# Attention block on one core: the loop's matmuls issued as two column tiles of 64

## The chip, the cores and the metric

The kernel runs on one core of a Trainium2 chip. The metric is the device time of one execution in microseconds (us); lower is better. The engines that matter are TensorE (PE, matmuls, with its weight loads listed apart as PEld), VectorE (DVE), ScalarE (ACT), GpSimd (POOL) and the queue of SyncE (SP), which here only issues DMAs. [...] A matmul holds one operand (the weights) in TensorE's array and streams the other (the moving operand) through it. The columns of the weights become the partitions of the result in PSUM. Each matmul in the program is a weight load and a matmul for the engine.

## What is computed

```
x (8, 112, 640), k_cache and v_cache (8, 32, 512, 192), wq (640, 6144), wo (6144, 640), all bf16
q = (x @ wq).reshape(B, Sq, H, Dh).transpose(0, 2, 1, 3)
scores = einsum("bhqd,bhkd->bhqk", q, k_cache) * Dh ** -0.5
p = softmax(scores)
o = einsum("bhqk,bhkd->bhqd", p, v_cache)
return o.transpose(0, 2, 1, 3).reshape(B, Sq, H * Dh) @ wo
```

## The kernel before

The work is cut into 128 pairs of heads: 4 groups of 8 heads, 8 batches in each, 4 pairs in each batch. A loop of periods runs over the pairs, and each engine has a fixed list of stages for a period, each with a lag, written out by hand (`DEFAULT_ORDERS`, lines 12 to 18). There is no scheduler: a stage waits on semaphores and then issues its instructions in order. For pair `i`, TensorE's list is S(i), PT0(i-1), PV(i-2), PT1(i-1), O(i-3), Q(i+2).

- **S** (`pe_S`, L166 to L169): scores of the two heads, four matmuls each. The weights are q (112 columns), the moving operand is a K tile with 256 elements a partition.
- **PT0, PT1** (`pe_PT`, L182): transposes the exponentials of one head and scales them, by four matmuls against a diagonal matrix `dg` (112 moving elements, 128 columns of weights).
- **PV** (`pe_PV`): the weights are V, the moving operand the transposed probabilities, 112 elements. A head has 192 channels. The first 128 run in L200 as full-width matmuls, eight a pair. The last 64 run in L206 with 64 columns: head 0 writes PSUM partitions 0 to 63, head 1 partitions 64 to 127, alternating, eight a pair.
- **O** (`pe_O`, L234 and L235): multiplies by wo, three times 512 and 128 moving elements, 112 columns of weights.
- **Q** (`pe_Q`, L262): projects x with wq for a later pair, 15 matmuls with 112 moving elements and 128 columns.

At the start `pe_xt` (L402) transposes x.

VectorE's list for a period: the scaled copy and row minimum of the scores of both heads (L332), four copies that lay q out (L323 to L326), the copy of one transposed head from PSUM (L338), reciprocals (L344), two diagonals (L308), and, once in four pairs, two instructions that add the output to `acc` (L373 to L377). ScalarE empties PSUM for Q, PT0 and PV (L272, L278, L291) and does the exponentials (L284).

K and V come from DRAM in 64 groups of four heads, that is of two pairs. SP issues them in turn: a transposing DMA for K (L477), then a DMA for V (L489). Each has six buffers. The K DMA of a group waits until the scores of the group six before it are done, the V DMA until PV of that group is. The weights wq and wo are issued by POOL, paced by waits on the K that has landed. [...]

An instruction carries a tile size and a tile position in the array. Before, all matmuls have the size 128x128, save those of L206: these have 128 rows by 64 columns, at column 0 or 64.

## Time and profile before

| | |
|---|---|
| time, median of 3 runs | 501.38 us (500.34 to 502.07) |
| span of the profiled execution | 499.2 us |
| granted TensorE clock, mean | 0.999 |
| matmuls, and as many weight loads | 6824 |
| ACT, share of the span busy | 71% |
| DMA moved | 119.90 MB, 240 GB/s in the mean |
| K transposes (L477), 64 | median 9.9 us from issue to landing |

A profile is one execution of the program, taken on the chip. The page gives busy times of each engine, a strip of the span in 40 slices, the DMA queues, the chain of waits that ended last, and the costliest groups of instructions. Matmuls are pipelined, so one matmul's listed duration, for example 213 ns in L200, is longer than the step to the next; steps are read from starts. In the list of groups, a row gives line, engine, operation, output and inputs, shapes, count, then total busy time and mean ns of one, then the idle time of the engine before them and what ended it. In the timeline, a row gives start and duration in us, engine, line, operation and how many were merged (x4). In the list of DMA queues the columns are packets, MB and share of 16 engines.

### The profile page before, as it was taken

To read this page: it belongs to the slowest core of one execution; us is meant where nothing else is said; L and a number is where in the kernel's file an instruction comes from. 1 tells how busy PE (TensorE), PEld (TensorE's weight loads), DVE (VectorE), ACT (ScalarE), POOL (GpSimd) and SP (SyncE) were. 2 spreads that over 40 slices of the span, in tenths; PEclk is the share of its full clock that TensorE was granted. 3 is DMA by queue.
4 is the path that set the end of the run, shared out by engine and by line. 5 is a ranking of instruction groups with operands and counts; after the bars stand their busy time and mean duration, and the time that the engine had idled before them with its cause. 6 is when DMAs were issued, how large, how long until landed. Compare 5 with 4: busy or idle time off the path is not lost.

```text
span 499.2 us, 18678 instructions
## 1 busy us (share of the span) xinstructions
PE 479.0 (96%) x6824; PEld 418.9 (84%) x6824; DVE 446.6 (89%) x1610; ACT 355.1 (71%) x898; POOL 71.5 (14%) x133
## 2 busy tenths in 40 slices
PE   1799999999999999999999999999999999999995
PEld 1788888888888888888888888888888888888884
DVE  2589999998999999999999999999999999999994
ACT  1277777777777777777777777777777777777773
POOL 7110133131000133131000122322000000000000
PEclk9999999999999999999999999999999999999999
DMA  9999999999999999999999999999999999999000
GB/s 227 305 285 239 244 256 274 249 265 292 237 249 263 281 261 259 245 265 251 239 247 236 259 290 279 240 282 260 233 272 254 255 260 255 238 258 261 3 14 25
DMA packets 239738, 119.90 MB, mean 240 GB/s; under 512 B 201840, under 2 KB 236480, under 8 KB 239648
## 3 DMA queue, kind: packets, MB, share of 16 engines
q1 hardware_dynamic: 233472, 101.82, 94.4%
q0 software_dynamic: 6176, 16.88, 11.3%
q8 instruction: 56, 0.92, 0.8%
q14 instruction: 34, 0.28, 0.2%
HBM read 67.21 MB, written 1.15 MB: 137 GB/s over the span
## 4 chain that ended last, share of the span: by engine, by line
PE 93%; DMA 2%; issue 1%; DVE 1%; POOL 1%; ACT 0%; DVEq 0%; POOLq 0%; ACTq 0%
PE ps L262 19%; PE ps L234 16%; PE ps L182 13%; PE ps L200 10%; PE ps L206 8%; PE ps L166 6%; PE ps L169 6%; PE ps L167 6%; PE ps L168 6%; PE ps L235 4%; DMA wq_sb<-in_wq_dram 2%; DVE xT_sb L409 1%; POOL wq_sb L578 0%; DVE s_sb L332 0%; DVE o_out L377 0%
## 5 line engine op out<-in xcount | busy, mean ns | idle before, releaser
L284 ACT ACTIVATE p_sb<-s_sb,nmx 112x512 bf16<-112x512 f32 x256 | 181.6, 712 | 3.1 <-DVE s_sb L332 2.1
L332 DVE TENSOR_SCALAR_CACHE_REDUCE s_sb<-ps 112x512 f32<-112x512 f32 x256 | 166.3, 686 | 16.2 <-PE ps L169 14.0
L278 ACT ACTIVATE pT_sb<-ps 128x448 bf16<-128x448 f32 x128 | 69.5, 543 | 88.4 <-PE ps L182 88.4
L262 PE MATMUL ps<-xT_sb,wq_sb 128*128 128x112 bf16 x1920 | 118.0, 215 | 5.2 <-DMA wq_sb<-in_wq_dram 5.2
L234 PE MATMUL ps<-wo_sb,oT_sb 128*112 128x512 bf16 x384 | 118.3, 380 | 0.0
L262 PEld LDWEIGHTS ps<-xT_sb,wq_sb 128*128 128x128 bf16 x1920 | 103.8, 99 | 16.7 <-DMA wq_sb<-in_wq_dram 4.4
L182 PE MATMUL ps<-dg,p_sb 112*128 112x112 bf16 x1024 | 94.0, 214 | 1.8 <-ACT p_sb L284 1.6
L272 ACT ACTIVATE qs<-ps 128x336 bf16<-128x336 f32 x128 | 57.6, 450 | 45.0 <-PE ps L262 41.8
L338 DVE CAST pT_sb<-ps 128x448 bf16<-128x448 f32 x128 | 79.9, 624 | 5.3 <-PE ps L182 1.4
L235 PE MATMUL ps<-wo_sb,oT_sb 128*112 128x128 bf16 x384 | 83.9, 219 | 0.0
L182 PEld LDWEIGHTS ps<-dg,p_sb 112*128 112x128 bf16 x1024 | 64.5, 98 | 14.4 <-ACT p_sb L284 1.9
L166 PE MATMUL ps<-kt,qs 128*112 128x256 bf16 x256 | 70.8, 277 | 2.5 <-issue 1.9
L200 PE MATMUL ps<-pT_sb,vt 128*128 128x112 bf16 x1024 | 71.8, 213 | 0.1
L167 PE MATMUL ps<-kt,qs 128*112 128x256 bf16 x256 | 70.4, 275 | 0.0
L169 PE MATMUL ps<-kt,qs 128*112 128x256 bf16 x256 | 70.4, 275 | 0.0
L168 PE MATMUL ps<-kt,qs 128*112 128x256 bf16 x256 | 70.3, 275 | 0.0
L234 PEld LDWEIGHTS ps<-wo_sb,oT_sb 128*112 128x112 bf16 x384 | 49.7, 129 | 22.3
L581 POOL DMA_DIRECT2D wq_sb<-in_wq_dram x60 | 32.1, 539 | 188.5 <-DMA kt<-in_k_cache_dram 182.4
L308 DVE TENSOR_SCALAR dg<-ident,rinv 112x112 bf16<-112x112 bf16 x256 | 52.9, 249 | 5.0 <-issue 0.5
L200 PEld LDWEIGHTS ps<-pT_sb,vt 128*128 128x128 bf16 x1024 | 56.5, 98 | 0.9 <-issue 0.5
L291 ACT ACTIVATE oT_sb<-ps 128x336 bf16<-128x336 f32 x128 | 55.3, 432 | 1.7 <-PE ps L206 1.7
L235 PEld LDWEIGHTS ps<-wo_sb,oT_sb 128*112 128x112 bf16 x384 | 50.0, 130 | 0.0
(38 smaller groups left out, 498.5 us busy)
## 6 DMA issues: line engine op xcount, KB each, us to landing
vt<-in_v_cache_dram SPq DMA_DIRECT2D x64, 768.0 KB, 5.8
wq_sb<-in_wq_dram POOLq DMA_DIRECT2D x60, 96.0 KB, 5.3
wo_sb<-in_wo_dram POOLq DMA_DIRECT2D x24, 160.0 KB, 5.6
wo_sb<-in_wo_dram POOLq DMA_DIRECT2D x32, 80.0 KB, 5.1
wq_sb<-in_wq_dram POOLq DMA_DIRECT2D x4, 480.0 KB, 10.2
wo_sb<-in_wo_dram POOLq DMA_DIRECT2D x4, 320.0 KB, 10.9
out_dram<-o_out SPq DMA_DIRECT2D x8, 140.0 KB, 4.4
kt<-in_k_cache_dram SPq DMA_TRANSPOSE x64, 9.9
```

What stands on the lines that cost most here:

```text
L166: pe.matmul(bk[:, 0:256], qs[:, qb, EA[h], :], ktb[:, :, 0, cs], start=True, stop=False)
L167: pe.matmul(bk[:, 0:256], qs[:, qb, ET[h], :], ktb[:, :, 1, cs], start=False, stop=True)
L168: pe.matmul(bk[:, 256:512], qs[:, qb, OC[h], :], ktb[:, :, 2, cs], start=True, stop=False)
L169: pe.matmul(bk[:, 256:512], qs[:, qb, OH[h], :], ktb[:, :, 1, cs], start=False, stop=True).then_inc(sS, 1)
L182: mm = pe.matmul(ps[:, 2 + h, j * SQ:(j + 1) * SQ], p_sb[:, pslot, j * 128:(j + 1) * 128], dg[:, dslot, :], start=True, stop=True)
L200: pe.matmul(ps[:, 4, oc * SQ:(oc + 1) * SQ], vtb[:, u, q * 192: q * 192 + 128], pT_sb[:, ptb, h, j * SQ:(j + 1) * SQ], start=(j == 0), sto ...
L234: pe.matmul(ps[0:SQ, 6, :], oT_sb[:, ob, c, :], wo_sb[:, wb, 3 * lp + c, 0:512], start=first, stop=last)
L235: mm = pe.matmul(ps[0:SQ, 7, 0:128], oT_sb[:, ob, c, :], wo_sb[:, wb, 3 * lp + c, 512:640], start=first, stop=last)
L262: mm = pe.matmul(ps[:, 5, c * SQ:(c + 1) * SQ], lhsT, xT_sb[:, dc, b * SQ:(b + 1) * SQ], start=(dc == 0), stop=(dc == DC - 1))
L284: act.activation(p_sb[:, Hh % NP, :], s_sb[:, Hh % NSS, :], ACTF.Exp, bias=nmx[:, Hh % NS:Hh % NS + 1], scale=-1.0, accum_out=rsum[:, Hh % ...
L332: dve.tensor_scalar(s_sb[:, Hh % NSS, :], ps[0:SQ, h, :], -scale, None, op0=ALU.mult, op1=ALU.min, accum_out=nmx[:, Hh % NS:Hh % NS + 1]). ...
L338: dve.tensor_copy(pT_sb[:, ip % NPT, 1, :], ps[:, 3, 0:4 * SQ]).then_inc(dPTE, 1)
```

## The change

A helper `mmc` issues a matmul as two: columns 0 to 63 of the weights into PSUM partitions 0 to 63, then the rest into the partitions from 64 on. Both have the same moving operand. It is used in S, PT0, PT1, the L200 part of PV, O and Q. Where the weights have 112 columns the second tile has 48, else 64. The alternating matmuls of L206 stay as they are, and so do the transposes at the start. The semaphore is still signalled by the last matmul of a stage. The program then has 12584 matmuls, all with tile size 128x64 but the 40 of the start. No other engine's code changes.

```diff
+        def mmc(pe, out, lhsT, rhs, start, stop, m):
+            for a in (0, 64):
+                e = min(a + 64, m)
+                mm = pe.matmul(out(a, e), lhsT(a, e), rhs, start=start, stop=stop)
+            return mm
...
-                bk = ps[0:SQ, h, :]
...
-                pe.matmul(bk[:, 0:256], qs[:, qb, EA[h], :], ktb[:, :, 0, cs], start=True, stop=False)
...
+                mmc(pe, lambda a, e: ps[a:e, h, 0:256], lambda a, e: qs[:, qb, EA[h], a:e], ktb[:, :, 0, cs], True, False, SQ)
...
-                mm = pe.matmul(ps[:, 2 + h, j * SQ:(j + 1) * SQ], p_sb[:, pslot, j * 128:(j + 1) * 128],
-                               dg[:, dslot, :], start=True, stop=True)
+                mm = mmc(pe, lambda a, e: ps[a:e, 2 + h, j * SQ:(j + 1) * SQ],
+                         lambda a, e: p_sb[:, pslot, j * 128 + a:j * 128 + e], dg[:, dslot, :], True, True, 128)
...
-                    pe.matmul(ps[:, 4, oc * SQ:(oc + 1) * SQ], vtb[:, u, q * 192: q * 192 + 128],
-                              pT_sb[:, ptb, h, j * SQ:(j + 1) * SQ], start=(j == 0), stop=(j == 3))
+                    mmc(pe, lambda a, e: ps[a:e, 4, oc * SQ:(oc + 1) * SQ],
+                        lambda a, e: vtb[:, u, q * 192 + a:q * 192 + e],
+                        pT_sb[:, ptb, h, j * SQ:(j + 1) * SQ], j == 0, j == 3, 128)
...
-                pe.matmul(ps[0:SQ, 6, :], oT_sb[:, ob, c, :], wo_sb[:, wb, 3 * lp + c, 0:512], start=first, stop=last)
-                mm = pe.matmul(ps[0:SQ, 7, 0:128], oT_sb[:, ob, c, :], wo_sb[:, wb, 3 * lp + c, 512:640], start=first, stop=last)
+                mmc(pe, lambda a, e: ps[a:e, 6, :], lambda a, e: oT_sb[:, ob, c, a:e],
+                    wo_sb[:, wb, 3 * lp + c, 0:512], first, last, SQ)
+                mm = mmc(pe, lambda a, e: ps[a:e, 7, 0:128], lambda a, e: oT_sb[:, ob, c, a:e],
+                         wo_sb[:, wb, 3 * lp + c, 512:640], first, last, SQ)
...
-                    lhsT = wq_sb[:, wb, dc, c0 + 128 * c:c0 + 128 * (c + 1)]
-                    mm = pe.matmul(ps[:, 5, c * SQ:(c + 1) * SQ], lhsT, xT_sb[:, dc, b * SQ:(b + 1) * SQ],
-                                   start=(dc == 0), stop=(dc == DC - 1))
+                    w0 = c0 + 128 * c
+                    mm = mmc(pe, lambda a, e: ps[a:e, 5, c * SQ:(c + 1) * SQ],
+                             lambda a, e: wq_sb[:, wb, dc, w0 + a:w0 + e], xT_sb[:, dc, b * SQ:(b + 1) * SQ],
+                             dc == 0, dc == DC - 1, 128)
```

More of the change, by code (lines that the diff above doesn't have):

```diff
@@ L162, in pe_S @@
                 W(pe, dSM, Hh - 1)
-                bk = ps[0:SQ, h, :]
                 ktb = kt[kb]
                 cs = slice(u * 128, (u + 1) * 128)
-                pe.matmul(bk[:, 0:256], qs[:, qb, EA[h], :], ktb[:, :, 0, cs], start=True, stop=False)
-                pe.matmul(bk[:, 0:256], qs[:, qb, ET[h], :], ktb[:, :, 1, cs], start=False, stop=True)
-                pe.matmul(bk[:, 256:512], qs[:, qb, OC[h], :], ktb[:, :, 2, cs], start=True, stop=False)
-                pe.matmul(bk[:, 256:512], qs[:, qb, OH[h], :], ktb[:, :, 1, cs], start=False, stop=True).then_inc(sS, 1)
+                mmc(pe, lambda a, e: ps[a:e, h, 0:256], lambda a, e: qs[:, qb, EA[h], a:e], ktb[:, :, 0, cs], True, False, SQ)
+                mmc(pe, lambda a, e: ps[a:e, h, 0:256], lambda a, e: qs[:, qb, ET[h], a:e], ktb[:, :, 1, cs], False, True, SQ)
+                mmc(pe, lambda a, e: ps[a:e, h, 256:512], lambda a, e: qs[:, qb, OC[h], a:e], ktb[:, :, 2, cs], True, False, SQ)
+                mmc(pe, lambda a, e: ps[a:e, h, 256:512], lambda a, e: qs[:, qb, OH[h], a:e], ktb[:, :, 1, cs], False, True, SQ).then_inc(sS, 1)
         def pe_PT(pe, ip, h):
```

## Prediction

> **What bounds the kernel now.** I read the engines' shares first, then the chain of waits, then TensorE, VectorE and the DMA queue in order of time.

> ```profile
> PE 479.0 (96%) x6824; PEld 418.9 (84%) x6824; DVE 446.6 (89%) x1610; ACT 355.1 (71%) x898; POOL 71.5 (14%) x133
> ...
> PE 93%; DMA 2%; issue 1%; DVE 1%; POOL 1%; ACT 0%; DVEq 0%; POOLq 0%; ACTq 0%
> ```

> TensorE (PE) is the chain, but two others stand close behind it: VectorE (DVE) is busy 89% of the span, and the DMA row is at 9 in nearly every slice. So what the change saves on PE has to be followed until one of these takes over. In steady state one pair of heads takes 3.65 us (starts of L166 lie at 252.81 and 256.46 in the timeline, and most of the 128 steps of the trace read 3.64 to 3.65). Here is the part of such a step that holds the mixed tilings, TensorE in order of time:

> ```profile
> 253.69 0.36 PE L182 MATMUL ps<-dg,p_sb 112*128 112x112 bf16 x4
> 253.88 0.56 PE L200 MATMUL ps<-pT_sb,vt 128*128 128x112 bf16 x8
> 254.38 0.39 PE L206 MATMUL ps<-pT_sb,vt 128*64 128x112 bf16 x8
> 254.69 0.37 PE L182 MATMUL ps<-dg,p_sb 112*128 112x112 bf16 x4
> 254.90 0.38 PE L234 MATMUL ps<-wo_sb,oT_sb 128*112 128x512 bf16 x1
> ```

> Read the starts, since the durations overlap. Four matmuls of L182 move on by 0.19 us, 49 ns each. Eight of L200 at 49 ns would be 0.39 us, but L206 starts 0.50 us later. L206 is the stage already in 64-column tiles, and the next lines show how it runs: the same eight matmuls asked for in windows that end 0.05 us apart.

> ```profile
> 254.38 0.24 PE L206 MATMUL ps<-pT_sb,vt 128*64 128x112 bf16 x2
> 254.38 0.29 PE L206 MATMUL ps<-pT_sb,vt 128*64 128x112 bf16 x4
> 254.38 0.34 PE L206 MATMUL ps<-pT_sb,vt 128*64 128x112 bf16 x6
> ```

> They start two at a time, and a pair costs what one full matmul does: the single records start at 254.375/.379, 254.449/.452, 254.498/.501 and 254.547/.550, so 49 ns a pair after a first step of 74 ns.

> **The cost of a tiling switch.** From the last L200 start (254.233) to the first L206 start (254.375) is 142 ns, 93 more than 49. The first pair's 74 ns is 25 more. From the last pair (254.547) to L182 (254.695) is 148 ns, 99 more. The step behind that, 60 ns (251.049 to 251.109 one turn earlier), is 11 more. Together 228 ns of each 3.647 us. Times 128 pairs that is 29 us, the most that the change can remove.

> **What the change adds on PE.** Each split matmul becomes two with half the columns and the same moving rows. Priced by L206 a pair at 112 moving elements is 49 ns, which is also the step of L182, L200 and L262. For 256, 512 and 128 moving elements I keep today's steps of 109, 215 and 55 ns, because they scale with the moving side, and that is unchanged. PE then needs 3.647 - 0.228 = 3.42 us a pair. Bounds of the pair's step: 49 ns from L206's second to fourth pair, 74 ns from its first, and below 49 nothing, as the moving side alone gives that in L182. I take 49, since it is the nearest row. The startup transposes of L402 stay on the full array: four changes of tiling, well under 1 us.

> Weight loads lie beside the matmuls:

> ```profile
> L262 PEld LDWEIGHTS ps<-xT_sb,wq_sb 128*128 128x128 bf16 x1920 | 103.8, 99 | 16.7 <-DMA wq_sb<-in_wq_dram 4.4 <-DVE xT_sb L409 1.8
> ...
> L167 PEld LDWEIGHTS ps<-kt,qs 128*112 128x112 bf16 x256 | 33.8, 132 | 0.0
> ...
> L206 PEld LDWEIGHTS ps<-pT_sb,vt 128*64 128x64 bf16 x1024 | 30.6, 109 | 11.6
> ```

> A 64-column load takes 109 ns against 99 for 128 columns, and 132 for 112. In L206 two such loads still fit under each 49 ns pair, so I cost them at nothing; the cover is the running pair, and without it every pair would pay some 10 ns. [...]

> Instructions on PE's queue grow from 106 to 196 a pair (53 to 98 matmuls with a load each), 17 ns each at 3.42 us. The trace's records of PE's own waits date the handing out: between one that ends at 257.463 and the next at 257.615 lie the 32 loads and matmuls of L200 and L206, so 4.8 ns each is possible, and the densest stages ask for 12.3 (49/4). No charge. [...]

> **What takes over: VectorE.** Its instructions are not touched.

> ```profile
> 253.14 0.88 DVE L375 TENSOR_TENSOR acc<-ps,acc 112x512 f32<-112x512 f32 x2
> 253.94 0.68 DVE L332 TENSOR_SCALAR_CACHE_REDUCE s_sb<-ps 112x512 f32<-112x512 f32 x1
> ...
> 257.25 0.68 DVE L332 TENSOR_SCALAR_CACHE_REDUCE s_sb<-ps 112x512 f32<-112x512 f32 x1
> ```

> From 253.94 to 257.25 DVE has no gap: 3.31 us is the least for a pair. Every fourth pair adds the sum into acc, 0.80 us (253.14 to 253.94) to 0.82. Four pairs need 4 x 3.31 + 0.82 = 14.06 us. PE needs 4 x 3.647 = 14.59 now and 13.68 after. So DVE becomes the bound at 14.06, 7.03 us for a group of two pairs (K and V come in groups of four heads), against 7.29 now. If nothing else held, 64 groups would win 64 x 0.265 = 17 us.

> **And the K stream.** K arrives by transposing DMAs on SP's queue:

> ```profile
> 331.22 7.15 SPq L477 DMA_TRANSPOSE kt<-in_k_cache_dram  x1
> 338.41 0.58 SPq L489 DMA_DIRECT2D vt<-in_v_cache_dram  x1
> 339.04 7.42 SPq L477 DMA_TRANSPOSE kt<-in_k_cache_dram  x1
> ```

> SP is back to back, 7.8 us a group here, slower than either engine will be. It doesn't wait for PE: group 46's buffer was given up by group 40's scores at about 319.4, 20 us before 339.04. So faster matmuls don't bring K sooner. By the trace's landing records, groups 10 to 14 land 0.4 us before PE starts on them (already PE's limit at 94 to 125 us); later the lead is 5 to 15 us and at the end 27. A group's start is the later of the last start plus the period, and landing plus 0.4. With 7.29 this recursion puts group 63 at 482.5 (trace: 483.5). With 7.03 it is held again around groups 30 and 45, lastly by group 46, landed at 351.2. From there on weight loads ease, K comes in about 6.1 us a group, and DVE decides.

> More PE instructions are fetched; their DMA queue is this row (packets, MB, share of 16 engines):

> ```profile
> q8 instruction: 56, 0.92, 0.8%
> ```

> The extra is 11,520 loads and matmuls at 13,648/56 = 244 a packet are 47 packets of 1.14 us (0.8% of 16 engines' 499.2 us, by 56), 3.4 us on 16 engines, 2.4 us of it before group 46. Bounds 0 (hidden) and 2.4 (the engines are full); I take 2.4, as the DMA row is at 9 there.

> **The sum.** 351.2 + 2.4 + 0.4 = 354.0 for group 46; 17 groups of 7.03 us to group 63 make 473.5; from there to the end 15.7 us now (499.2 - 483.5), less two pairs' switches 0.4: span 488.8. The runs' median lies 2.2 us above the profiled span (501.38 to 499.2), so 491.0 us. Its own range: no fetch cost and PE's 6.84 us a group give 485, a full period of 7.1 us and the uncut tail give 494.

> **Rivals.**
> 1. *The gain arrives whole.* If K lands earlier than in this one trace, DVE's bound alone gives 501.4 - 17 = 484, and PE's 29 us would give 472. For: the three runs spread by 1.7 us, so something outside PE varies. Against: back-to-back SP issue until 455 us.
> 2. *Slower: twin tiles don't keep 49 ns in long rows.* L206 shows four pairs only, just behind a drain in which the queue filled up. After the change the same load of two weight tiles per pair runs 15 pairs long in L262 and 20 long from L182 to L182. If a pair takes the 74 ns of L206's first, 35 pairs a step cost 0.875 us and regain 0.228: 128 x 0.65 = +83, 584 us. The change decides at 228/35 = 6.5 ns a pair, 55.5 ns. Against: three even steps of 49 ns.
> 3. *Slower: instructions come too slowly.* At 24.6 ns each (49/2, the densest that a row of 30 shows in L262) a pair takes 196 x 24.6 = 4.82 us, 128 x 1.17 = +150, 651 us. Against: the 4.8 ns above.
> 4. *No change.* K's stream would have to be 11 us late at group 46, 3%; fetches give 2.4.
> 5. *The switches stay,* because a 48-column piece is another tiling. The second pieces start at partition 64 as L206's do, so I give it nothing of its own; it would land with 2 or 4.

> **Chances.** Forecast 0.70, rival 1 0.08, rival 2 0.12, rival 3 0.04, rivals 4 and 5 0.06. Of this kernel's three runs, 0.3% (1.5 us) is about what can be told from no change. Faster 0.79, same 0.05, slower 0.16. 481 to 500 holds the forecast, half of rival 1 and most of the small losses of gain between; rivals 2 and 3 lie beyond it.

> **What would show it.** Gaps of 142 and 148 ns around L206 gone, every split stage in twins 49 ns apart per pair; DVE without idle time before L332 in stretches of 14.06 us per four pairs; PE idle before the first matmul of the scores, on K, in groups near 10 to 14, 30 and 45; K's last landing still at 457 to 461. Wrong would be: a pair step above 55 ns, PE idle on "issue" all along, or VectorE's operations longer than now while two tiles write.

## The result and the profile after

| | before | changed |
|---|---|---|
| time, median of 4 runs each | 500.86 us (499.67 to 502.07) | 656.25 us (649.98 to 660.28) |
| span of the profiled execution | 499.2 us | 648.2 us |
| granted TensorE clock, mean | 0.999 | 0.945 |
| instruction DMAs of TensorE's queue (16 KB each) | 56 | 101 |

The changed kernel is slower: the ratio is 1.307, with an interval of 1.302 to 1.312. The ratio leaves out the slowest run of the changed kernel, which is 1.6% above its fastest. The forecast was 491 us.

From the page of the changed kernel: busy times, the strip of the granted clock, TensorE's instruction DMAs, and the chain of waits.

```profile
PE 488.6 (75%) x12584; PEld 439.1 (68%) x12584; DVE 449.1 (69%) x1610; ACT 355.1 (55%) x898; POOL 71.4 (11%) x133
...
PEclk9899988988887899888999989999899999999999
...
q8 instruction: 101, 1.65, 1.1%
...
PE 69%; issue 24%; DVE 4%; DMA 2%; POOL 1%; ACT 0%; DVEq 0%; POOLq 0%; ACTq 0%
```

TensorE is busy only 75% of a span 149 us longer. In the chain "issue" stands at 24%, time in which an engine waits for nothing that the profile shows. Before it was 1%. The prediction had named this as a sign of being wrong. Who waited for whom (us in total, times, longest) says the same:

```profile
PEld ps L156 <- issue: 150.3, 89, 6.2
PE ps L156 <- issue: 134.1, 57, 6.1
```

All split matmuls now have the helper's line, L156. They stood still without a semaphore, 57 times, up to 6.1 us.

Did the array do what the change says? TensorE in order of time, in a stretch without such a stop (L212 is the old L206):

```profile
326.74 0.36 PE L156 MATMUL ps<-dg,p_sb 112*64 112x112 bf16 x8
326.94 0.56 PE L156 MATMUL ps<-pT_sb,vt 128*64 128x112 bf16 x16
327.33 0.36 PE L212 MATMUL ps<-pT_sb,vt 128*64 128x112 bf16 x8
327.53 0.36 PE L156 MATMUL ps<-dg,p_sb 112*64 112x112 bf16 x8
```

Starts move on by 0.20, 0.39 and 0.20 us: four, eight and four pairs of tiles at 49 ns, with no gap around L212. Steps without a stop take 3.42 us. So the switches are gone, and split pairs cost what whole matmuls did. The loss is all between the matmuls. Here is one such place, TensorE in order of time:

```profile
296.67 0.95 PE L156 MATMUL ps<-xT_sb,wq_sb 128*64 128x112 bf16 x30
300.91 0.85 PE L156 MATMUL ps<-kt,qs 128*64 128x256 bf16 x8 [3.29 <-issue]
```

The DMA strip of the stretch 297.4 to 300.9 us (40 slices of 88 ns) and its queues:

```profile
DMA  9999999999999999908000110010000099999000
...
q1 hardware_dynamic: 2144, 0.54, 115.6%
q8 instruction: 1, 0.02, 1.8%
```

Until about 299 us the DMA engines are full of K's packets. One packet of q8, TensorE's instructions, falls into the stretch: by its record it starts at 298.36, ends at 299.34, and 1.56 us later the matmuls go on. And busy times before, in and behind the stop (columns: window, its length, PE, PEld, DVE, ACT and POOL busy, then the granted clock, DMA share and GB/s):

```profile
293.32:297.40 4.08, 4.08 (x124) 3.88 (x125) 2.81 (x10) 2.54 (x7) 0.00 (x0) 1.00 1.19 288
297.40:300.90 3.50, 0.22 (x9) 0.07 (x3) 0.62 (x4) 0.64 (x2) 0.00 (x0) 1.00 1.17 159
300.90:304.40 3.50, 3.49 (x58) 3.33 (x60) 2.17 (x8) 1.37 (x4) 0.00 (x0) 0.54 0.02 5
```

Behind the stop the clock is 0.54 for 3.5 us, so about half as many matmuls get through: 58 in 3.50 us (16.6 a us) against 124 in 4.08 us (30.4 a us).

**What the stops have in common.** Counting TensorE's records from the start (loads, matmuls and its wait instructions), 58 of the 59 gaps over 0.6 us (from one matmul's start to the next, after 35 us) end at an instruction number that leaves 193 or 194, once 195, when divided by 256. A packet of q8 has 16 KB, and 101 of them for 25,882 records work out at 256 instructions of 64 bytes a packet. The queue follows TensorE: its records were 14,362 before, with 56 packets, while the page's other instruction queue, q14, has 34 packets in both kernels. In each of the 58 the matmuls go on 1.2 to 1.7 us after the end of the packet that holds their block. The 59th, 1.8 us near the end, waits for the last exponentials and is in the profile before too. The 58 sum to 151 us.

### The profile page after: what moved, and what is told of

It is laid out like the page before. It is cut to its first block, busy times and chain, and to the rows that moved or that the text cites. A ratio compares the mean times of both kernels' runs of the same rounds, so it can differ in the third digit from the quotient of the medians.

```text
span 648.2 us, 30198 instructions
## 1 busy us (share of the span) xinstructions
PE 488.6 (75%) x12584; PEld 439.1 (68%) x12584; DVE 449.1 (69%) x1610; ACT 355.1 (55%) x898; POOL 71.4 (11%) x133
## 4 chain that ended last, share of the span: by engine, by line
PE 69%; issue 24%; DVE 4%; DMA 2%; POOL 1%; ACT 0%; DVEq 0%; POOLq 0%; ACTq 0%
PE ps L156 65%; PE ps L212 4%; DMA wq_sb<-in_wq_dram 2%; DVE s_sb L341 1%; DVE pT_sb L347 1%; DVE xT_sb L418 0%; DVE qs L334 0%; DVE qs L335 0%; ACT p_sb L293 0%; POOL wq_sb L587 0%; DVE dg L317 0%; DVE rinv L353 0%; DVE o_out L386 0%; DVE qs L333 0%; DVE qs L332 0%
## 5 line engine op out<-in xcount | busy, mean ns | idle before, releaser
L341 DVE TENSOR_SCALAR_CACHE_REDUCE s_sb<-ps 112x512 f32<-112x512 f32 x256 | 167.6, 688 | 119.3 <-PE ps L156 118.8
L156 PE MATMUL ps<-xT_sb,wq_sb 128*64 128x112 bf16 x3840 | 131.0, 220 | 58.9 <-issue 53.5
L156 PE MATMUL ps<-kt,qs 128*48 128x256 bf16 (+1 forms) x2048 | 146.3, 283 | 24.0 <-issue 23.3
L156 PEld LDWEIGHTS ps<-xT_sb,wq_sb 128*64 128x64 bf16 x3840 | 115.2, 115 | 72.4 <-issue 59.1
L156 PE MATMUL ps<-wo_sb,oT_sb 128*48 128x512 bf16 (+3 forms) x1536 | 139.1, 313 | 9.6 <-issue 9.6
L156 PEld LDWEIGHTS ps<-kt,qs 128*48 128x48 bf16 (+1 forms) x2048 | 112.3, 111 | 29.5 <-issue 27.4
L156 PE MATMUL ps<-dg,p_sb 112*64 112x112 bf16 x2048 | 107.9, 221 | 28.7 <-issue 26.9
L156 PEld LDWEIGHTS ps<-dg,p_sb 112*64 112x64 bf16 x2048 | 87.6, 116 | 31.0 <-issue 28.9
L156 PEld LDWEIGHTS ps<-wo_sb,oT_sb 128*48 128x48 bf16 (+1 forms) x1536 | 76.4, 112 | 35.2 <-issue 15.6
L156 PE MATMUL ps<-pT_sb,vt 128*64 128x112 bf16 x2048 | 82.2, 220 | 20.8 <-issue 20.8
L156 PEld LDWEIGHTS ps<-pT_sb,vt 128*64 128x64 bf16 x2048 | 67.3, 116 | 19.4 <-issue 19.3
L212 PE MATMUL ps<-pT_sb,vt 128*64 128x112 bf16 x1024 | 53.8, 221 | 7.9 <-issue 7.9
L212 PEld LDWEIGHTS ps<-pT_sb,vt 128*64 128x64 bf16 x1024 | 39.7, 116 | 11.5 <-issue 11.5
```

The source lines that it names most:

```text
L156: mm = pe.matmul(out(a, e), lhsT(a, e), rhs, start=start, stop=stop)
L212: mm = pe.matmul(ps[64 * h:64 * h + 64, 4, SQ:2 * SQ], vtb[:, u, q * 192 + 128: q * 192 + 192], pT_sb[:, ptb, h, j * SQ:(j + 1) * SQ], sta ...
L341: dve.tensor_scalar(s_sb[:, Hh % NSS, :], ps[0:SQ, h, :], -scale, None, op0=ALU.mult, op1=ALU.min, accum_out=nmx[:, Hh % NS:Hh % NS + 1]). ...
```

## The experiments

The table is worked out from the traces. "Block" is how long 256 instructions last at the kernel's full pace: with the waits counted, TensorE executes 112 instructions a pair before and 202 after, so 256/112 x 3.65 and 256/202 x 3.42 (the expectations say 4.46 us for the latter, without the waits). "Wait" is the time from the first instruction of a block to the start of the DMA that brings the next one, median and maximum over the run. After that come about 1.1 us of transfer and at least 1.2 us until the block runs. "Gaps" are steps of over 0.6 us from one matmul's start to the next after 35 us, number and sum.

| kernel | block, us | wait, us | gaps | time, us |
|---|---|---|---|---|
| before | 8.3 | 3.5, 6.3 | 1, 1.8 us | 500.9 |
| changed | 4.3 | 3.7, 8.3 | 59, 152.9 us | 656.3 |
| e1, changed, K's DMAs left out | 4.3 | 1.5, 6.1 | 18, 30.4 us | 512.5 |
| e2, changed, V's DMAs left out | 4.3 | 2.0, 7.4 | 31, 56.9 us | 546.2 |
| e5, changed, K's and V's left out | 4.3 | 0.9, 5.4 | 3, 6.5 us | 494.3 |
| e6, before, K's and V's left out | 8.3 | 0.5, 4.0 | 1, 1.8 us | 499.3 |
| e3, cut untiled, 202 loads and matmuls | 4.7 | 3.1, 9.0 | 50, 116.8 us | 672.6 |
| e7, cut untiled, 140 loads and matmuls | 6.5 | 3.7, 5.8 | 22, 25.8 us | 531.7 |
| e4, changed, K in four DMAs | 4.3 | 3.1, 6.5 | 60, 116.5 us | 606.6 |
| e8, PV untiled | 8.3 | 3.4, 6.1 | 2, 2.6 us | 498.7 |

**Is it the DMA traffic? e1, e2, e5 and e6.** The edits, on the changed kernel (e6: both, on the kernel before; e1, e5 and e6 also pace the weight loads by the scores):

```diff
-            W(pe, mK[kb], 16 * (g // NKB + 1))
+            W(pe, mK[kb], 16)
...
-                        issue_k(g)
+                        if g < NKB:
+                            issue_k(g)
```

```diff
-            W(pe, mV[vb], 16 * (g // NVB + 1))
+            W(pe, mV[vb], 16)
...
-                    if 0 <= g - VLAG < NGRP:
+                    if 0 <= g - VLAG < NVB:
```

> The changed kernel without K's traffic: K is loaded for the first six groups only, and later scores use those tiles again (the weight loads are paced by the scores instead of by K's landing). Theory 1, TensorE's instruction blocks (16 KB, 256 instructions, 4.46 us of work) wait behind K's bursts of 256-byte packets: a block then arrives in about 1.2 + 1.1 + 1.3 = 3.6 us, the stalls of 1 to 6 us at every 256th instruction go, the clock stays at 1.0, and VectorE's 14.06 us per four pairs is the bound: 475 to 500 us. Theory 2, a block takes some 6 us whatever else the DMA engines do: 620 to 660 us. Theory 3, two column tiles are slow in themselves or throttle the clock: also 600 us or more, but with long steps inside the stages, not with stalls at block ends.

Measured: 512.5 us, ratio 1.023 (1.017 to 1.028) to the kernel before in the same runs. Theories 2 and 3 fall. It is 12 us above theory 1's range, because 30 us of gaps are left, 11 us of that before 62 us, while the first loads run.

> The changed kernel without V's traffic after the first six groups (PV uses those tiles again); K stays. If it is K's 256-byte bursts that hold a block back, little changes: 600 to 650 us, stalls still of 2 to 3 us on average. If any DMA load does it, in proportion to bytes (V is 42% of what is moved), half of the stalls go: 530 to 590 us.

Measured: 546.2 us, ratio 1.090 (1.076 to 1.103). Leaving out V alone takes away almost two thirds of the gaps. So it is not K's small packets alone that hold the blocks back; both streams do, K's more.

> The changed kernel without K's and V's traffic: both are loaded for the first six groups only and used again. If other DMA traffic is all that holds instruction blocks back, stalls at block ends are gone once the first groups are in (under 15 us in all), and VectorE bounds: run e1 showed 3 x 3.42 + 3.90 = 14.16 us per four pairs, 32 times is 453, with 25 to 35 us of start and end 478 to 490 us. If a block takes a fixed time of its own that is too long for 196 instructions a pair, no better than e1: 505 to 520 us.

> The kernel before without K's and V's traffic, as the partner of e5. TensorE bounds at 3.647 us a pair: 128 x 3.647 = 467, with the same start and end 490 to 500 us. So the two switches are worth 8 to 15 us (VectorE caps it) when instructions come in time. If the tiles themselves cost something, e5 is not below this.

Measured: e5 494.3 us, ratio 0.987 (0.983 to 0.990); e6 499.3 us, ratio 0.998 (0.995 to 1.000). With K and V out of the DMA engines' way the same matmuls have 3 gaps instead of 59. The change is then worth 5 us against e6, less than the 8 to 15 expected, and e5 lies 4 us above its range: its third to eighth steps take 9.4 us longer than e6's, while the first loads run. Behind them VectorE is the bound, seen in e5 in order of time (every instruction between these is left out; none is preceded by idle time put down to a releaser):

```profile
297.21 0.28 DVE L384 TENSOR_TENSOR acc<-ps,acc 112x128 f32<-112x128 f32 x1
297.40 0.68 DVE L341 TENSOR_SCALAR_CACHE_REDUCE s_sb<-ps 112x512 f32<-112x512 f32 x1
...
311.43 0.28 DVE L384 TENSOR_TENSOR acc<-ps,acc 112x128 f32<-112x128 f32 x1
311.63 0.68 DVE L341 TENSOR_SCALAR_CACHE_REDUCE s_sb<-ps 112x512 f32<-112x512 f32 x1
```

From L341 to the L341 four pairs later are 14.23 us. TensorE's steps in most of the run, read at the starts of Q, are 3.42, 3.42, 3.42 and 3.90, 14.16 us.

**Is it the tiles, or the number of instructions? e3 and e7.** Both take the kernel before, with its two switches, and cut matmuls along the moving side, so that no column tile is added. e7 has only the cuts of the scores and of O; e3 also has the three like the third here:

```diff
-                pe.matmul(bk[:, 0:256], qs[:, qb, EA[h], :], ktb[:, :, 0, cs], start=True, stop=False)
...
+                for a in (0, 128, 256, 384):
...
+                    pe.matmul(bk[:, a:a + 128], qs[:, qb, lo[h], :], ktb[:, v, md, cs], start=True, stop=False)
...
-                pe.matmul(ps[0:SQ, 6, :], oT_sb[:, ob, c, :], wo_sb[:, wb, 3 * lp + c, 0:512], start=first, stop=last)
+                for v in range(4):
+                    pe.matmul(ps[0:SQ, 6, v * 128:v * 128 + 128], oT_sb[:, ob, c, :], wo_sb[:, wb, 3 * lp + c, v * 128:v * 128 + 128],
...
-                mm = pe.matmul(ps[:, 2 + h, j * SQ:(j + 1) * SQ], p_sb[:, pslot, j * 128:(j + 1) * 128],
-                               dg[:, dslot, :], start=True, stop=True)
+                for v in (0, 56):
+                    mm = pe.matmul(ps[:, 2 + h, j * SQ + v:j * SQ + v + 56], p_sb[:, pslot, j * 128:(j + 1) * 128],
+                                   dg[:, dslot, v:v + 56], start=True, stop=True)
```

> The kernel before, with no column tile added (the two switches a pair stay), but its matmuls cut along the moving side: scores and O into pieces of 128, PT, the wide part of PV and Q into 56. 202 loads and matmuls a pair, against 106 before and 196 in the change. TensorE needs at least 3.647 + 0.046 + 31 x 2.4 ns = 3.77 us a pair, more if weight loads don't fit under 26 ns. Theory 1: a block of 256 lasts only 4.8 us, stalls at every second block or so as in the change, 610 to 690 us. Theory 3 (the column tiles are to blame): no stalls at block ends, 512 to 530 us, or above that only by longer steps in the stages of 56.

Measured: 672.6 us, ratio 1.342 (1.330 to 1.354). TensorE in order of time, Q and the first scores, without a stop:

```profile
501.74 0.94 PE L270 MATMUL ps<-xT_sb,wq_sb 128*128 128x56 bf16 x30
502.51 0.24 PE L170 MATMUL ps<-kt,qs 128*112 128x128 bf16 x1
```

Thirty matmuls of 56 move on by 0.77 us, 26 ns each: the array's work costs little more (a step without a stop is 3.81 us, against 3.65 before). The waits of its engine:

```profile
PE ps L270 <- issue: 36.9, 20, 3.7
PE ps L205 <- issue: 19.0, 7, 6.6
PE ps L186 <- issue: 16.8, 9, 3.9
```

The same stops as in the changed kernel, 49 of 50 at the same place of a block, with full tiles in these lines. Column tiles are not the cause.

> The kernel before with only the scores and O cut into pieces of 128 moving elements: 140 loads and matmuls a pair, no column tile added. TensorE needs 3.647 + 0.046 = 3.69 us a pair, and a block of 256 lasts 6.75 us, between 8.8 before and 4.46 in the change. Starvation by blocks (theory 1) is a matter of degree: some blocks come late, 10 to 30 stalls, 10 to 45 us: 515 to 550 us. Were it only the number of instructions handed out a second, 140 in 3.69 us (26 ns each) would pass without loss: 504 to 510 us.

Measured: 531.7 us, ratio 1.062 (1.056 to 1.067), with 22 gaps. It is a matter of degree, as theory 1 had it: a block of 6.5 us comes too late only when its wait exceeds about 4 us.

**Would shorter bursts help? e4.**

```diff
-                sp.dma_start_transpose(dst, src).then_inc(mK[kb], 16)
+                for t in range(4):
+                    c = slice(t * 128, (t + 1) * 128)
+                    sp.dma_start_transpose(dst[:, :, c], src[c, :]).then_inc(mK[kb], 16)
```

> The changed kernel with each group's K transpose issued as four DMAs, one a head. Theory 1 with the burst as the unit: a block waits for a quarter of today's burst at most, under 2 us, and most stalls go: 487 to 530 us. If a block instead waits until K's queue is empty, or takes 6 us anyway, nothing changes: 620 to 660 us.

Measured: 606.6 us (598.9 and 614.2; the trace, and so the table's row, is of the latter). Neither expectation holds: the gaps fall from 153 to 117 us and the median wait from 3.7 to 3.1 us, far less than to a quarter. What exactly the block's DMA stands behind (one burst, a queue of several, V and the weights as well) is left open.

**A way without more instructions: e8.** The last 64 channels of V run as full tiles too, 128 columns starting 64 earlier for the second head, and ScalarE picks the valid halves:

```diff
+                    c0 = (2 * ip + h) % G * 768 + QJ[j] * 192 + 128 - 64 * h
+                    mm = pe.matmul(ps[:, 4, h * SQ:(h + 1) * SQ], vf[:, c0:c0 + 128],
...
+            act.activation(oT_sb[0:64, ob, 1, :], ps[0:64, 4, 0:112], ACTF.Copy)
+            act.activation(oT_sb[64:128, ob, 1, :], ps[64:128, 4, 112:224], ACTF.Copy).then_inc(aPVE, 1)
```

> The other way to a tiling that never changes, with no instruction added on TensorE: the last 64 channels of PV run as full-width matmuls too (128 columns of V, of which half the rows of the result are used), and ScalarE empties them with three instructions instead of one. Eight steps of 49 ns take the place of four twin steps and 228 ns of switches: 392 against 424 ns, 32 ns a pair, 4.1 us. Instructions stay at 106 a pair, so no stalls. 496 to 499 us, if K's stream and ScalarE's extra 0.28 us a pair (busy 71% before) leave it visible; 500 to 502 if not.

Measured: 498.7 us against 500.7, ratio 0.9961 (0.9942 to 0.9979): 2.0 us faster than the kernel before, the best of all that kept the whole computation. TensorE in order of time:

```profile
301.14 0.55 PE L200 MATMUL ps<-pT_sb,vt 128*128 128x112 bf16 x8
301.53 0.56 PE L206 MATMUL ps<-pT_sb,vt 128*128 128x112 bf16 x8
301.92 0.36 PE L182 MATMUL ps<-dg,p_sb 112*128 112x112 bf16 x4
```

Two stages of eight in 0.39 us each, no switch; steps are 3.62 us. 128 pairs by 0.03 us is 4 us, of which half arrives; from 95 to 126 us TensorE still waits for K (groups 10 to 14 start 0.09 us after their K lands, with steps up to 4.4 us).

## Why the prediction was wrong

**The step that failed** is "More PE instructions are fetched", and with it "No charge" for the queue. I counted the packets well (47 more; 45 came), but priced them as load on the DMA engines: 47 by 1.14 us over 16 engines, 3.4 us, of which the sum took 2.4. They are a wait on TensorE's own path. Judged by the starts of the fetches, the next block is asked for about when the current one begins (no fetch of the changed kernel starts earlier than 0.04 us before that, none of any run earlier than 0.81 us), waits for its DMA as long as other traffic makes it, and needs 2.3 us more. That latency didn't change (median wait 3.5 us before, 3.7 after). What changed is the time that covers it: 8.3 us a block before, 4.3 after. My evidence, 4.8 ns an instruction between two wait records, was right and beside the point: it shows how fast instructions within a block are handed out. Why the next block is not asked for earlier, no run shows.

The size closes to 3 us from the parts: 499.2 - 29 (128 x 0.228 of switches) + 151 (stops) + 30 = 651, against a span of 648.2. The 30 us are the clock: 16 stretches, 71.7 us of the span, were granted at half speed, and 61.0 us of them lie outside the gaps, which costs about half of that (16.6 matmuls a us against 30.4 above). The sum of the prediction had no term for the clock.

**Point by point.** The switches: right, 3.42 us a step as worked out. Twin tiles at 49 ns, with weight loads of 64 columns (114 to 116 ns each in the list) hidden: right (rival 2 is refuted; the 48-column pieces of rival 5 cause no switch). VectorE as the next bound: right, 14.16 to 14.23 us in e5 against 14.06, but it never came to bear in the changed kernel. The K stream as the cap: not tested there, since TensorE fell behind it; in the kernel before, taking K and V away won 1.5 us (interval 0 to 2.5; e6), so the waits on K were worth little at the old pace. One reading was off: by L166 groups 10 to 14 start 0.09 us after their K lands, and the prediction's 0.4 us holds for L169, the last matmul of a head's scores; its sum goes by L169 at both ends (483.5 us for group 63), so nothing moves by it. Rival 3 gave 651 us, close to the result, but by another mechanism: a slow pace of 24.6 ns for each instruction, where the trace has 17 ns within a block and stops between blocks. Its 0.04 was too little: I had looked at the pace alone and never asked how far ahead a block is fetched, though the instruction DMAs' own records in the trace before gave the answer: blocks that run 8.3 us, and waits up to 6.3 us for the next one, with 2.3 more to come.

## What to carry to other kernels

Before adding instructions to TensorE, divide: how long do 256 of them (a block in these traces) last, and how long does the instruction DMA take in this kernel's traffic, from the start of one block until the next can run? In the changed kernel, with full DMA engines, that was 6 us as a rule (3.7 + 1.1 + 1.2) and over 10 at worst (8.3 + 2.3), against 4.3 us that a block lasted, and TensorE stopped at 58 block ends, although each instruction cost only 17 ns within a block. Where a tiling switch is the target, look first for a form with as many instructions as before (e8, 2.0 us faster).
